# Residuals from GpSimd to VectorE, and value products by column halves, in a fused attention, expert and MLP kernel

## The chip, the cores and the metric

One Trainium2 chip; the kernel runs on one core. The metric is device time in microseconds (us) of one execution. The engines are PE (TensorE matmul, with its weight loads as PEld), DVE (VectorE), ACT (ScalarE), POOL (GpSimd) and SP (SyncE, which issues DMAs).

## The reference

```python
# attention: q, k, v (2, 8, 576, 64)
scores = scale * np.matmul(q, k.transpose(0, 1, 3, 2))        # scale 1/8
psi_rel = np.log1p(np.abs(rel)); psi_i = np.log1p(np.maximum(pos[:, None], 1.0))
h = np.maximum((psi_rel / psi_i)[..., None] @ w1 + b1, 0.0)   # w1 (1, 32)
scores = scores + (h @ w2).transpose(2, 0, 1)[None]           # w2 (32, 8): one bias per head
attn = softmax(scores); x = attn @ v                          # to (1152, 512)
# top-1 experts: 8 experts, capacity 288, 512 -> 1024 -> 512
expert_idx = np.argmax(x @ w_gate, axis=1); gate_w = probs[np.arange(N), expert_idx]
# the first 288 tokens of each expert, in order: out[i] = gate_w[i] * (relu(x_e @ w1[e]) @ w2[e])
# MLP: 512 -> 2048 -> 512
h = x @ w_in; g = np.maximum(0.01 * h, h); return g @ w_out
```

All inputs are fp32, except that the MLP's weights come as 64-bit floats.

## The kernel before

**Pairs of high and low part.** Fp32 products are made from PE's fp32r format. A matrix is stored as a pair: a cast to fp32r (the high part) and the residual, the raw value minus its cast. Three kinds of pair matter here. `prep_k` (L229 to L240) makes a key tile K: one ACT cast (L235) of 64 rows, then two residual instructions (L238) into the other 64 rows. `prep_q` (L258 to L269) makes a query tile Q for one pair of heads; a letter of the string `QE` says which engines: A is ACT cast (L261) and POOL residual (L269), B is ACT cast and DVE residual (L266), C is DVE cast (L263) and POOL residual, D is both on DVE. `KHE` says the same for the four key tiles of the first batch: A is POOL, D is DVE. `wsplit` (L670 to L672) makes a weight block P of 128x1024: ACT cast (L671), then the residual (L672) on the engine that the call names.

**Attention.** The work is cut in units (b, c, p): batch, chunk of 128 query rows (c = 0 to 3, and the short chunk c = 4 with 64 rows, named NFULL) and pair of heads p. The ten (b, c) follow a list: (0,1), (0,0), (0,3), (1,3), (0,4), (0,2), (1,2), (1,1), (1,0), (1,4), with four p each, so n runs from 0 to 39. In iteration n PE makes the scores of unit n+1 (`qk`, L329, into the one PSUM tile St), the transposes of unit n (L362 to L368) and the value products of unit n-1 (`pv`). DVE adds the bias and takes the minimum (`ttr`, L341, called bias step below), ACT makes the exponential (L352), ACT or DVE copy the transposes out (L372 to L387). In the first 28 iterations the bias itself is made beside that: relus on ACT, DVE and POOL (L165 to L169), bias matmuls (L182), their copies (L193 on ACT, L195 on DVE), then a round through DRAM.

**Value products.** For a full chunk `pv` has, per key tile, two matmuls with 64 weight columns, one per head (L399). For the short chunk both heads' 64 query rows stand side by side in the moving operand, and one matmul with 128 weight columns per key tile makes all four quadrants (L402, the last key tile in L404), of which the two on the diagonal are used (`fin_a`).

**Other work of attention's end.** At n = 20 to 25 the conversion of MLP weights runs on DVE (`conv_op`: L685, L687, L689, three steps per block). At n = 36 and 37 the first two expert weight blocks are split by `wsplit`.

**Experts and MLP.** Two full blocks of tokens come first, the first with splits on DVE, the last (`big_last`, L1063) on POOL. Then the MLP runs over the tokens (`chunk`, L1206): 16 weight blocks in the order of `PO`, four up, four down, four up, four down. In an up step (`up_half`) PE makes the product (L856 to L858), ACT scales by 0.01 (L880), DVE takes the maximum (L881), ACT casts the result to hq (L888) and DVE makes its residual (L889). Between them DVE converts the weights of a later block (`next(cv)`, into the tile raw), and `wsplit` splits the block of two steps later. In a down step PE runs L1191 to L1193. Only the first call, `chunk(0, True)`, runs for these inputs, and `any_block` doesn't run.

Each engine runs its instructions in the order in which they are written in the program; where an instruction's input is not there, all that stands behind it on that engine waits.

Of the kernel before, what the change touches and what calls it, by code (L numbers as in the profile page):

```python
# [26 lines left out]
NFULL = S // 128  # L27
# [30 lines left out]
START = ["Q0 k0 k1", "q0 v0", "q1 K0 v1", "q2", "Q1 q3 v2", "", "K1", "k2", "v3 B3 k3", "", "", "", ""]  # L58
SG = ()
PX = ((),(0,1),(2,3),(),())  # L60
KHE = "ADAA"
RENG = ('DAAA', 'DADD', 'DAPD', 'DDDD', 'DDPA', 'DDAD')
RP = "355355535352525234144534444144444342"
EP = "111111111100011111111101110111111111"
TP = "0021211100000230323333333232021010103333"
VL, KL, KP = ((9, 9, 13, 12), (8, 9, 9, 10), (9, 10, 10, 11))
LA = 5
QE = "DACDCDDCCCCCCCCCDDDADADADADACADADCDCDDDD"
PF = (3, 8, 1, 14, 21, 28)
QUOTA = [2, 2, 2, 2, 2, 2, 2, 2, 2, 2, 1, 1, 1, 1, 1, 1, 1, 1, 1, 1, 1, 1, 1, 1, 2, 2, 1, 1]  # L70
CST_W = MO + 128 + 128 + 2 * E_N + NENT + 3
# [3 lines left out]
def tile_attention_moe_mlp(ctx, tc, qc, kc, vc, wpk, cst, ctok, cap, wm, wo, out):  # L75
    nc = tc.nc
# [314 lines left out]
    def pv(c, p, ATs, Vs, xp):  # L391
        V, vt, vd = Vs
        AT, AX_ = ATs
        if c < NFULL:
            for t in range(NFULL + 1):
                for j in range(2):
                    h = 2 * p + j
                    w, a = (V[:, t, 64 * h : 64 * h + 64], AT[:, j, 128 * t : 128 * t + 128]) if t < NFULL else (vd[:, p, 64 * j : 64 * j + 64], AX_)
                    nc.tensor.matmul(xp[64 * j : 64 * j + 64, p, :], w, a, start=t == 0, stop=t == NFULL)  # L399
        else:  # L400
            for t in range(NFULL):
                nc.tensor.matmul(xp[:, p, :], V[:, t, 128 * p : 128 * p + 128], AT[:, 0, 128 * t : 128 * t + 128],  # L402
                                 start=t == 0, stop=False)
            nc.tensor.matmul(xp[:, p, :], vt[:, 128 * p : 128 * p + 128], AX_[0:64], start=False, stop=True)  # L404

    def fin_a(c, rs, xp, last):
        xt = rt.tile([128, NP, 128], F32, name="xt", tag="xt", bufs=1)
# [256 lines left out]
    raws, Ps, xhls, regs = [], [], [], {}  # L664
# [95 lines left out]
    def hooks(n):  # L760
        if n == 1:
            setup_late()
        if n == 12:
            nc.vector.tensor_copy(capf, cpi[:, 0:1])
        if n in PF:
            prefill(srt, 3 * PF.index(n), 3)
        if n == 16:
            nc.sync.dma_start(sid.rearrange("(p a) c -> p a c", p=128), pat)
        if n == NB0 + 4:
            queue("acc0", route_acc(0, range(NCH)))  # L770
        if n == NB0 + 5:
            flush("acc0")
            queue("route0", route0())
            queue("first0", first0())
        if n == SC[0]:
            flush("route0")
        if n in SC:
            scatter(0, SC.index(n))
        if n in ACC1:
            queue("acc1", route_acc(1, [i for i in range(NFULL) if ACCN[i] == n]))  # L780
        if n - 1 in ACC1:
            flush("acc1")
        if n == RF + 1:
            flush("first0")
            regs["e0"] = nc.values_load(ints[0:1, 2:3], engines=[SP], min_val=0, max_val=E_N - 1)
            regs["x0"] = nc.values_load(ints[0:1, 3:4], engines=[SP], min_val=0, max_val=S)
        if n in (CV0 - 3, CV0 - 2, CV0 - 1):
            g_w64(n - CV0 + 3)
        k, odd = divmod(n - CV0 - 2, 2)
        if odd == 0 and 0 <= k < len(CVA):  # L790
            nc.sync.dma_start(wsc[CVA[k]], cvd[k])
            if k + 3 < len(CVA):
                g_w64(k + 3)
        if n == 36:
            for t, m in xtiles:
                if t % 2 == 0:
                    kr = p1.tile([128, 2, S], F32, name="x0r", tag="kr", bufs=KRB)
                x0.append(kr[:, t % 2, 0:DM])
                nc.sync.dma_start(x0[t][0:m], srt[sl_(regs["x0"] + 128 * t, m), 0:DM])
            copy_id(regs["x0"], 0, CAPB)  # L800
        if n in (33, 34, 36, 37):
            raws.append(wp.tile([128, 1024], F32, name="raw", tag="bs", bufs=5))
            wdma(wsrc(regs["e0"], len(raws) - 1), raws[-1])
        if n in (36, 37):
            Ps.append(wp.tile([128, 2, 1024], F32R, name="P", tag="G", bufs=3))
            wsplit(raws[n - 36], Ps[-1], nc.gpsimd)
        if n == 38:
            xhls.append(wp.tile([128, 2, NP, CAPB], F32R, name="xhl0", tag="G", bufs=3))
        if n in (38, 39):
            wdma(wsrc(regs["e0"], n - 34), raws[n - 38])  # L810
        if n >= 38:
            x_tr(n - 38, x0[n - 38], xhls[0])
        if n == N:
            route1a()
            scatter(1, 0)
            scatter(1, 1)

    def tail_part(fa):
# [243 lines left out]
        def big_last():  # L1062
            xbase, base = bval(0, 1, 1, [SP]), bval(0, 1, 2, [ACT, DVE, SP])  # L1063
            copy_id(xbase, base, CAPB)
            ne = bval(1, 0, 0, [SP])
            for j in range(8):
                big_step(j, base, nc.gpsimd)
                if j > 2:
                    wdma(wsrc(ne, j - 3), R8[j - 3])

# [133 lines left out]
        def chunk(c, first):  # L1204
            w = MCS[c]
            groups = [(t, min(128, w - 128 * t)) for t in range(-(-w // 128))]  # L1206
            cv = convs()
            PP = [Ds[i] if first and i < 2 else Ps[i % 4] for i in range(16)]
            if not first:
                for i in range(3):  # L1210
                    wdma(wsc[i], raws[i])
                yprep(c)
            for i in range(3, 5):
                conv_start(i)
            if not first:
                for i in range(2):
                    wsplit(raws[i], PP[i], nc.vector)
            for i in range(13):
                if i + 2 < 16:
                    wsplit(spare if first and i == 0 else raws[(i + 2) % 4], PP[i + 2], nc.gpsimd)  # L1220
                q = PO[i]
                if q < 8:
                    for g in (0, 2, 1, 3):
                        up_half(PP[i], 2 * q + g // 2, w // 2 * (g % 2), w // 2)
                        if g != 3:
                            next(cv, None)
                else:
                    for kk in range(2):
                        for t, n in groups:
                            down_tok(PP[i], 2 * (q - 8) + kk, t, n)  # L1230
                            if t == 0:
                                split_h()
                            if 2 * t + kk in DCV:
                                next(cv, None)
                if i == 5:
                    for t, n in groups:
                        nc.sync.dma_start(idg[0:n, t], sid[MOF[c] + 128 * t : MOF[c] + 128 * t + n].bitcast(I32))
            wsplit(raws[15 % 4], PP[15], nc.vector)
            for t, n in groups:
                for i in range(13, 16):  # L1240
                    for kk in range(2):
                        down_tok(PP[i], 2 * (PO[i] - 8) + kk, t, n)
                emit(t, n)
# [21 lines left out]
    for n in range(N + 1):  # L1265
# [9 lines left out]
        if n + 1 < N:  # L1275
            b, c, p = units[n + 1]
# [88 lines left out]
```

## Time and profile before

| | |
|---|---|
| median of 3 runs | 407.12 us (406.49 to 407.96) |
| profiled execution | 408.05 us, of which the span is 406.3 |
| PE busy | 375.9 us, 93% of the span |
| PEld busy | 312.6 us, 77% |
| DVE busy | 307.7 us, 76%, 733 instructions |
| ACT busy | 242.9 us, 60% |
| POOL busy | 139.1 us, 34%, 110 instructions |
| PE's granted clock | full but for three stretches, two of them inside the work |

By stage: attention to about 214 us, the experts to 282, the chunk to the end. From about 244 on PE is busy in 9 tenths or more of nearly every slice of the page. A row of a timeline gives the start, the duration, the engine, the line, the operation, out and in, the number of instructions, and in brackets how long the engine had been idle before and what ended that.

### The profile page before, as it was taken

How to read it: one execution, taken by the hardware profiler on the slowest of the kernel's cores; microseconds unless marked ns; L12 is line 12 of the kernel's file. 1: busy time of each engine (PE TensorE's matmuls, PEld its weight loads, DVE VectorE, ACT ScalarE, POOL GpSimd, SP SyncE). 2: the span in 40 equal slices, each digit the busy share in tenths (PEclk: the TensorE clock that was granted, in tenths of full speed). 3: DMA queues.
4: the chain of work that ended last, by engine and by line, in shares of the span. 5: the costliest groups of instructions: out<-in, count | busy, mean ns of one | idle time of the engine just before them, and what ended most of it. 6: DMA issues, size and time to landing. Idle time of an engine off the chain costs nothing. (4 is left out here: it accounts for less than half of the span.)

```text
span 406.3 us, 8427 instructions
## 1 busy us (share of the span) xinstructions
PE 375.9 (93%) x2990; PEld 312.6 (77%) x2990; DVE 307.7 (76%) x733; ACT 242.9 (60%) x522; POOL 139.1 (34%) x110
## 2 busy tenths in 40 slices
PE   4777999988999999999999999999999999899993
PEld 2234666756688888988889999998988778788872
DVE  5998989899854888899458972137899999999310
ACT  3857898788865878767654875556544222455100
POOL 1445857574101110212332206840242255222311
PEclk9999899999999999999998999999999999999997
DMA  7979599798879938889185299683243366530011
GB/s 180 320 235 322 157 330 313 274 297 250 216 236 262 353 135 233 224 253 250 46 236 201 69 327 343 217 289 114 106 173 127 106 207 206 209 106 2 19 59 51
DMA packets 34050, 81.79 MB, mean 201 GB/s; under 512 B 8427, under 2 KB 8811, under 8 KB 31952
## 3 DMA queue, kind: packets, MB, share of 16 engines
q1 hardware_dynamic: 32880, 78.70, 61.3%
q0 software_dynamic: 1120, 2.48, 1.7%
q8 instruction: 25, 0.41, 0.4%
q14 instruction: 25, 0.20, 0.2%
HBM read 59.11 MB, written 23.20 MB: 203 GB/s over the span
## 5 line engine op out<-in xcount | busy, mean ns | idle before, releaser
L341 DVE CUSTOM_DVE_ANT_0 sv<-St,bt 128x576 f32<-128x576 f32 x72 | 52.9, 750 | 30.8 <-PE St L329 18.8
L672 POOL TENSOR_TENSOR P<-raw,P 128x1024 fp32r<-128x1024 f32 x18 | 45.3, 2521 | 76.6 <-ACT P L671 63.5
L352 ACT ACTIVATE A<-sv,mx 128x576 f32<-128x576 f32 x72 | 59.3, 837 | 3.2 <-DVE mx L341 3.0
L329 PE MATMUL St<-K,Q 128*128 128x320 f32 (+1 forms) x320 | 53.6, 310 | 2.6 <-DVE mx L341 2.2
L329 PEld LDWEIGHTS St<-K,Q 128*128 128x128 f32 x320 | 43.9, 189 | 14.6 <-issue 8.4
L182 PE MATMUL pb<-Gt,WP 128*32 128x272 f32 (+17 forms) x352 | 42.1, 505 | 13.3 <-DVE Gt L165 7.5
L269 POOL TENSOR_TENSOR Q<-qr,Q 128x256 fp32r<-128x256 f32 x22 | 16.9, 769 | 99.9 <-ACT Q L261 62.1
L165 DVE TENSOR_SCALAR Gt<-WL,bp 128x400 f32<-128x400 f32 (+17 forms) x98 | 49.4, 563 | 0.1
L671 ACT CAST P<-raw 128x1024 fp32r<-128x1024 f32 x27 | 28.3, 1048 | 28.3 <-DVE raw L689 22.7
L362 PE MATMUL pt<-CS,A 128*128 128x128 f32 x288 | 41.5, 284 | 1.3 <-ACT A L352 0.8
L372 ACT COPY AT<-pt 128x512 f32<-128x512 f32 x40 | 23.3, 583 | 29.2 <-PE pt L362 28.9
L362 PEld LDWEIGHTS pt<-CS,A 128*128 128x128 f32 x288 | 38.1, 206 | 2.2 <-ACT A L352 1.3
L169 POOL TENSOR_SCALAR Gt<-WL,bp 128x528 f32<-128x528 f32 (+12 forms) x17 | 34.1, 2009 | 8.2 <-DVE Gt L165 7.3
L399 PE MATMUL xp<-AT,V 128*64 128x128 f32 x512 | 35.9, 284 | 0.0
L399 PEld LDWEIGHTS xp<-AT,V 128*64 128x64 f32 x512 | 28.0, 139 | 9.8 <-issue 9.5
L182 PEld LDWEIGHTS pb<-Gt,WP 128*32 128x32 f32 x352 | 12.4, 110 | 29.8 <-DVE Gt L165 14.7
L856 PE MATMUL g<-yhl,P 128*128 128x304 f32 x96 | 30.5, 318 | 3.9 <-DVE gfa L881 3.9
L193 ACT ACTIVATE bs<-pb,CS 128x288 f32<-128x288 f32 (+53 forms) x60 | 27.2, 500 | 10.1 <-PE pb L182 9.5
L1193 PE MATMUL ac<-P,hq 128*128 128x512 f32 (+1 forms) x80 | 31.5, 394 | 0.0
L1191 PE MATMUL ac<-P,hq 128*128 128x512 f32 (+1 forms) x80 | 31.5, 394 | 0.0
L1192 PE MATMUL ac<-P,hq 128*128 128x512 f32 (+1 forms) x80 | 31.5, 394 | 0.0
L889 DVE TENSOR_TENSOR hq<-gfa,hq 128x304 fp32r<-128x304 f32 x32 | 28.9, 902 | 1.4 <-ACT hq L888 1.4
(322 smaller groups left out, 907.4 us busy)
## 6 DMA issues: line engine op xcount, KB each, us to landing
bt<-scr SPq DMA_DIRECT2D x24, 576.0 KB, 6.0
w<-wo SPq DMA_DIRECT2D x13, 1024.0 KB, 5.0
scr<-bs SPq DMA_DIRECT2D x36, 295.5 KB, 4.2
raw<-wm SPq DMA_DIRECT2D x14, 512.0 KB, 6.2
w<-wm SPq DMA_DIRECT2D x10, 512.0 KB, 5.7
srt<-pre SPq DMA_DIRECT2D x6, 771.0 KB, 8.4
qr<-qc SPq DMA_DIRECT2D x16, 256.0 KB, 5.7
w64g<-wo SPq DMA_DIRECT2D x3, 1024.0 KB, 10.3
```

Of the source, the lines that this page charges most:

```text
L165: nc.vector.tensor_scalar(G, src, bp[:, g : g + 1], 0.0, op0=ALU.add, op1=ALU.max)
L169: nc.gpsimd.tensor_scalar(G, src, bp[:, g : g + 1], 0.0, op0=ALU.add, op1=ALU.max)
L182: nc.tensor.matmul(pb[32 * q : 32 * q + 32, 0 : hi - lo], W2, gs[:, q, lo:hi], start=True, stop=True)
L329: nc.tensor.matmul(St[:, o + lo : o + hi], Q[:, h - 2 * p, w, :], K[:, h - 2 * p, lo:hi], start=n == 0, stop=n == len(seq) - 1)
L341: nc.vector.tensor_tensor_reduce(out=sv, in0=St, in1=bt[:, jb], scale=-0.125, scalar=3.0e38, op0=ALU.add, op1=ALU.min, accum_out=mx)
L352: nc.scalar.activation(A[:, :, j], sv, AF.Exp, bias=mx, scale=-1.0, accum_out=rs[:, col : col + 1])
L362: nc.tensor.transpose(pt[:, 128 * t : 128 * t + 128], A[:, 128 * t : 128 * t + 128, j], ident)
L399: nc.tensor.matmul(xp[64 * j : 64 * j + 64, p, :], w, a, start=t == 0, stop=t == NFULL)
L672: eng.tensor_tensor(out=P_[:, 1], in0=raw, in1=P_[:, 0].bitcast(F32), op=ALU.subtract)
L1191: nc.tensor.matmul(ps, hh, wh, start=k == 0, stop=False)
L1192: nc.tensor.matmul(ps, hh, wl, start=False, stop=False)
L1193: nc.tensor.matmul(ps, hl, wh, start=False, stop=k == F2 // 128 - 1)
```

## The change

The strings `KHE` and `QE` move residuals of keys and queries from POOL to DVE: three of the four key tiles (two instructions each) and 22 query tiles, 8 of which (A to B) stay behind an ACT cast and 14 (C to D) behind a DVE cast. Three calls of `wsplit` or its user name DVE in place of POOL: the two blocks at n = 36 and 37, the eight of the last full block, 13 in the chunk. POOL keeps its share of the bias relus, memsets, copies of tokens and DMAs. And the short chunk's `pv` has two matmuls per key tile, one per head, with 64 weight and 64 moving columns, into the two quadrants that are used. Lines from L403 on have a number higher by 2 afterwards.

```diff
-KHE = "ADAA"
+KHE = "DDDD"
...
-QE = "DACDCDDCCCCCCCCCDDDADADADADACADADCDCDDDD"
+QE = "DBDDDDDDDDDDDDDDDDDBDBDBDBDBDBDBDDDDDDDD"
...
         else:
-            for t in range(NFULL):
-                nc.tensor.matmul(xp[:, p, :], V[:, t, 128 * p : 128 * p + 128], AT[:, 0, 128 * t : 128 * t + 128],
-                                 start=t == 0, stop=False)
-            nc.tensor.matmul(xp[:, p, :], vt[:, 128 * p : 128 * p + 128], AX_[0:64], start=False, stop=True)
+            for t in range(NFULL + 1):
+                for j in range(2):
+                    r = slice(64 * j, 64 * j + 64)
+                    h = slice(128 * p + 64 * j, 128 * p + 64 * j + 64)
+                    w, a = (V[:, t, h], AT[:, 0, 128 * t + 64 * j : 128 * t + 64 * j + 64]) if t < NFULL else (vt[:, h], AX_[0:64, r])
+                    nc.tensor.matmul(xp[r, p, r], w, a, start=t == 0, stop=t == NFULL)
...
         if n in (36, 37):
-            wsplit(raws[n - 36], Ps[-1], nc.gpsimd)
+            wsplit(raws[n - 36], Ps[-1], nc.vector)
...
             for j in range(8):
-                big_step(j, base, nc.gpsimd)
+                big_step(j, base, nc.vector)
...
                 if i + 2 < 16:
-                    wsplit(spare if first and i == 0 else raws[(i + 2) % 4], PP[i + 2], nc.gpsimd)
+                    wsplit(spare if first and i == 0 else raws[(i + 2) % 4], PP[i + 2], nc.vector)
```

DVE at the front, around the third key tile: the query pair of a later unit (L263, L266), two bias copies (L195) and relus (L165) ahead of the bias step of the next unit (L341). Before:

```order
L387 COPY AX__427<-pt_424 128x128
L263 CAST Q<-qr 128x2x128
L266 TENSOR_TENSOR Q<-qr,Q 128x2x128
L195 TENSOR_SCALAR bs<-pb,CS 128x512
L195 TENSOR_SCALAR bs<-pb,CS 128x79
L165 TENSOR_SCALAR Gt<-WL,bp 128x480 x3
```

and after:

```order
L387 COPY AX__427<-pt_424 128x128
L263 CAST Q<-qr 128x2x128
L266 TENSOR_TENSOR Q<-qr,Q 128x2x128
L238 TENSOR_TENSOR K<-kr,K 64x576 x2
L195 TENSOR_SCALAR bs<-pb,CS 128x512
L195 TENSOR_SCALAR bs<-pb,CS 128x79
L165 TENSOR_SCALAR Gt<-WL,bp 128x480 x3
```

The two key residuals, which need ACT's cast L235, stand ahead of the bias copies and relus.

DVE beside the conversion (tile cvo) in attention. Before:

```order
L685 TENSOR_SCALAR cvo<-w64g 128x1024
L479 RECIPROCAL xn<-tm 64x1
L415 TENSOR_SCALAR rs<-rs 128x8
L687 SCALAR_TENSOR_TENSOR cvo<-w64g,cvo 128x1024
L417 RECIPROCAL rec<-rs 128x8
L341 ISA sv,mx<-St,bt 128x576
```

and after, with the same lines now two higher:

```order
L687 TENSOR_SCALAR cvo<-w64g 128x1024
L266 TENSOR_TENSOR Q<-qr,Q 128x2x128
L417 TENSOR_SCALAR rs<-rs 128x8
L689 SCALAR_TENSOR_TENSOR cvo<-w64g,cvo 128x1024
L419 RECIPROCAL rec<-rs 128x8
L341 ISA sv,mx<-St,bt 128x576
```

The query residual, behind an ACT cast, stands ahead of the second conversion step and of the bias step.

DVE in an up step of the chunk, between two blocks' conversions (tile raw). Before:

```order
L689 SCALAR_TENSOR_TENSOR raw<-w_3172,raw 128x1024
L881 TENSOR_TENSOR gfa<-g_3189,gfa 128x304
L889 TENSOR_TENSOR hq_3175<-gfa,hq_3173 128x304
L881 TENSOR_TENSOR gfa<-g_3190,gfa 128x304
L889 TENSOR_TENSOR hq_3175<-gfa,hq_3173 128x304
L685 TENSOR_SCALAR raw<-w_3171 128x1024
```

and after:

```order
L691 SCALAR_TENSOR_TENSOR raw<-w_3212,raw 128x1024
L883 TENSOR_TENSOR gfa<-g_3229,gfa 128x304
L891 TENSOR_TENSOR hq_3215<-gfa,hq_3213 128x304
L674 TENSOR_TENSOR P_3210<-raw,P_3210 128x1024
L883 TENSOR_TENSOR gfa<-g_3230,gfa 128x304
L891 TENSOR_TENSOR hq_3215<-gfa,hq_3213 128x304
L687 TENSOR_SCALAR raw<-w_3211 128x1024
```

The weight residual (now L674) stands one pair of maximum and residual behind the conversion's last step, ahead of the next pair.

## Rows read from the trace of the kernel before

**Rows 1.** Stretches: length, busy us (x) of PE, PEld, DVE, ACT, POOL; PEclk, DMA, GB/s

```profile
40.00:45.00 5.00, 4.96 (x37) 2.50 (x38) 4.96 (x13) 3.56 (x9) 4.90 (x4) 0.66 0.61 200
...
80.00:90.00 10.00, 8.50 (x94) 5.99 (x94) 9.93 (x26) 9.34 (x20) 7.74 (x7) 1.00 1.01 302
...
130.00:140.00 10.00, 10.00 (x74) 9.22 (x74) 6.88 (x25) 7.97 (x23) 1.21 (x2) 1.00 0.89 307
...
282.70:313.40 30.70, 28.71 (x192) 27.01 (x193) 28.00 (x42) 16.70 (x38) 9.61 (x4) 1.00 0.42 153
...
341.20:371.70 30.50, 28.52 (x194) 26.94 (x193) 29.98 (x39) 14.58 (x32) 10.28 (x4) 1.00 0.40 140
```

**Rows 2.** Groups by line and form: busy us, mean ns | idle before, releasers

```profile
L672 POOL TENSOR_TENSOR P<-raw,P 128x1024 fp32r<-128x1024 f32 x18 | 45.3, 2521 | 76.6 <-ACT P L671 63.5 <-DVE raw L685 7.0 <-PE ac L1193 6.0
...
L672 DVE TENSOR_TENSOR P<-raw,P 128x1024 fp32r<-128x1024 f32 x9 | 10.9, 1219 | 3.0 <-ACT P L671 1.8 <-DMA out<-pre 1.2
...
L266 DVE TENSOR_TENSOR Q<-qr,Q 128x256 fp32r<-128x256 f32 x18 | 7.6, 424 | 0.3
...
L238 DVE TENSOR_TENSOR K<-kr,K 64x576 fp32r<-64x576 f32 x2 | 1.4, 748 | 0.1
```

**Rows 3.** Timeline of the chunk: start, us, engine, what, [idle before <-releaser]

```profile
301.28 1.05 ACT L671 CAST P<-raw 128x1024 fp32r<-128x1024 f32 x1 [1.12 <-DVE raw L689]
...
301.51 0.45 DVE L889 TENSOR_TENSOR hq<-gfa,hq 128x304 fp32r<-128x304 f32 x1
...
302.41 2.40 POOL L672 TENSOR_TENSOR P<-raw,P 128x1024 fp32r<-128x1024 f32 x1 [5.95 <-ACT P L671]
...
303.08 2.06 DVE L889 TENSOR_TENSOR hq<-gfa,hq 128x304 fp32r<-128x304 f32 x1
```

**Rows 4.** Groups of the weight conversion's third step, two tiles

```profile
L689 DVE SCALAR_TENSOR_TENSOR raw<-w,raw 128x1024 uint32<-128x1024 uint32 x13 | 24.1, 1857 | 0.2
...
L689 DVE SCALAR_TENSOR_TENSOR cvo<-w64g,cvo 128x1024 uint32<-128x1024 uint32 x3 | 3.6, 1214 | 0.0
```

**Rows 5.** Waits: us in total, times, longest; then PE at the first phase's end

```profile
PEld g L856 <- DVE gfa L881: 6.7, 13, 1.2
...
312.31 0.30 PE L857 MATMUL g<-yhl,P 128*128 128x304 f32 x1
...
313.42 0.39 PE L1191 MATMUL ac<-P,hq 128*128 128x512 f32 x1
```

**Rows 6.** Timeline of the last units of attention

```profile
200.73 1.05 ACT L671 CAST P<-raw 128x1024 fp32r<-128x1024 f32 x1
...
201.11 0.76 DVE L341 CUSTOM_DVE_ANT_0 sv<-St,bt 128x576 f32<-128x576 f32 x1 [1.99 <-PE St L329]
...
205.36 0.76 DVE L341 CUSTOM_DVE_ANT_0 sv<-St,bt 128x576 f32<-128x576 f32 x1 [2.54 <-PE St L329]
```

**Rows 7.** Timeline beside the conversion in attention

```profile
147.41 0.44 ACT L261 CAST Q<-qr 128x256 fp32r<-128x256 f32 x1
...
147.95 0.76 DVE L341 CUSTOM_DVE_ANT_0 sv<-St,bt 128x576 f32<-128x576 f32 x1 [0.25 <-ACT Q L261]
```

**Rows 8.** Timeline of the front

```profile
36.53 0.95 DVE L195 TENSOR_SCALAR bs<-pb,CS 128x512 f32<-128x512 f32 x2
...
37.46 1.15 ACT L235 CAST K<-kr 64x1152 fp32r<-64x1152 f32 x1 [2.28 <-DMA kr<-kc]
...
40.04 1.75 PE L182 MATMUL pb<-Gt,WP 128*32 128x480 f32 x8 [2.11 <-ACT bs L193]
...
40.43 0.74 DVE L341 CUSTOM_DVE_ANT_0 sv<-St,bt 128x576 f32<-128x576 f32 x1
```

**Rows 9.** Timeline of value products, PE and its weight loads

```profile
129.81 1.06 PE L402 MATMUL xp<-AT,V 128*128 128x128 f32 x8
...
148.88 0.85 PEld L399 LDWEIGHTS xp<-AT,V 128*64 128x64 f32 x16 [0.17 <-issue]
...
148.88 1.09 PE L399 MATMUL xp<-AT,V 128*64 128x128 f32 x16
```

## The prediction

> **What bounds the kernel now.** I read the table of busy time by stretch first, because the mean over the span (PE 93%, DVE 76%, POOL 34%) mixes stages with different limits. In the attention stretch 130 to 140 us PE is busy all of the 10.00 us and DVE 6.88 [rows 1]: there a shorter matmul step is worth its whole length and a DVE instruction is free. In 80 to 90 it is the other way round: DVE 9.93, PE 8.50 [rows 1]. In the expert chunk, between 282.7 and 313.4 and between 341.2 and 371.7, PE is at 28.71 of 30.70 and 28.52 of 30.50 and DVE at 28.00 and 29.98 [rows 1]: neither is free, and in the second of them DVE is as good as full. The busy time of DVE is then to be taken apart, since part of it is not work. The second view, the groups of instructions by line, gives each operation's price on either engine [rows 2]. The third, the timeline of the chunk, shows what DVE's figure hides: the residual of hq (L889) takes 0.45 us at 301.51, but 2.06 at 303.08, when POOL's residual (L672) runs from 302.41 for 2.40 [rows 3]. It ends at 305.14, just after POOL's end at 304.81. The weight conversion shows the same: L689 takes 1214 ns in the group whose tile is cvo and 1857 in the group whose tile is raw; 13 x 0.643 = 8.4 us more in all [rows 4]. So a DVE instruction with its operands in SBUF waits for a POOL residual to end, and pays nearly its whole length.
>
> The Trainium skill (SBUF — State Buffer, "Who interferes with whom") calls the port pair that DVE and GpSimd share an exclusive lock; the two rows of L889 agree, with 0.45 and 2.06 us. By it every move from POOL to DVE would be a gain wherever DVE works anyway, the early residuals too, which I do not take over, because those wait for ScalarE.
>
> **The change part by part.**
>
> Weight residuals, 23 that run: 13 in the chunk, 8 in the last full block, 2 in the last units of attention. On POOL one is 2.52 us in the mean, on DVE 1.22 [rows 2]. In the chunk, first up phase, four POOL residuals lie over it. Worked through at the one of 302.41: the cast on ACT begins at 301.28 and takes 1.05 [rows 3], so the residual can start on DVE at 302.33; the pair of sum and residual of hq ahead of it (the L889 of 301.51) is through at 301.96, so DVE waits 0.4; the residual lasts to 303.55 and the next pair, two instructions like the one of 0.45, to 304.5, against 305.14 now: 0.65 an instance, 2.6 in four. PE's weight loads wait 6.7 us for the sum gfa (L881) in 13 waits, and eight matmuls take 1.11 us at full rate (312.31 to 313.42), 0.139 each [rows 5]. With 192 matmuls per phase the floor is 26.7; the phase takes 30.7, so at most 4.0 can go. I take 1.7 of the 2.6, since the sum behind the moved residual comes later than now within its step. In the down phase between them PE sets the pace; DVE loses 8.4 us [rows 4] and so begins the second up phase late. Four residuals of 1.22 put 4.9 in place of 8.4: DVE arrives 3.5 earlier. In the second up phase DVE is full [rows 1], so this and its own smaller stretches come through, up to PE's floor, 30.5 - 26.7 = 3.8. I take 3.3. Chunk: -5.0, between -6.5 (most of 4.0 + 3.8) and -1.5 (below). What is late next there is the ACT cast (L671, 1.05), for which the DVE residual now has to wait in line, with the sums of the chunk behind it.
>
> The 8 residuals of the last full block: the first full block has its splits on DVE already, and from about 244 us on PE is busy in 9 tenths of nearly every slice, so 9.8 us more on DVE find room; I take 0, with +-0.5.
>
> The two residuals at n = 36 and 37 now stand on DVE ahead of two bias steps (L341). The first cast runs at 200.73 for 1.05 and ends at 201.78; the residual then ends at 203.0, while the bias step behind it had begun at 201.11 [rows 6]: 1.9 late. The exponential and then the next cast follow it on ACT, so that lag passes to the second residual, which stands ahead of the bias step of 205.36 [rows 6]. PE's transposes wait for those steps, but DVE had itself been idle 2.54 before 205.36, waiting for PE, so I take half: +1.0, between 0 and +2 (1.9, rounded). This also swallows what the value products gain in these units.
>
> Query residuals, 22 at 0.42 on DVE [rows 2] = 9.3 us. The 14 behind DVE's own cast cost only their length: in the written order four of them stand in the stretch that 80 to 90 stands for, where DVE is the bound, 1.7 us; POOL's query residuals no longer hold DVE there, by up to their own length each, which I set against it: 0, between -1 and +1. Eight stand behind a cast on ACT. Three of these meet a weight conversion: the cast at 147.41 runs 0.44, to 147.85, and the bias step begins at 147.95, with a conversion step of 1.21 [rows 4] already done [rows 7]. In the new order the residual comes before that conversion step, so DVE stands until 147.85 and does 0.42 + 1.21 before the bias step: near 149.5 instead of 147.95, 1.6 late. Three times is 4.8; PE has other units' work in between and I take 1.5 in all, between 0 and +3.
>
> Key residuals, six instructions at 0.75 [rows 2]: three tiles. The third shows the danger. DVE reaches it about 36.5, behind a query residual, where it now starts L195 (36.53) [rows 8]. The ACT cast for this tile, which itself waited for its load, begins at 37.46 and takes 1.15, to 38.61; two residuals bring DVE to 40.1, and L195, the bias relus and the bias step at 40.43 come 2.7 to 3.6 later. PE was idle 2.11 just before 40.04 [rows 8] and ran at a granted clock of 0.66 on average between 40 and 45 (half rate for most of it) [rows 1], so some of this lag falls into time already lost, and in the PE-bound stretch behind it DVE catches up. I take +1.0 for the three tiles, between 0 and +4.6 (rival 1).
>
> Value products of the short chunk, eight units (four in the stretch of 130, four near 205). Before, 8 records of 128 weight columns take 1.06 us (129.81) [rows 9]; after, 16 records of 64 weight columns and 64 moving columns. The same count with 128 moving columns (L399) takes 1.09 on PE and 0.85 in its weight loads (148.88) [rows 9]. A unit is between -0.5 (half of everything, 0.53) and +0.03 (L399's own time), and the switch of output quadrants, which no row of before prices, I bound by one record of the 16, +0.07. Nearest is L399, whose weights have the same size; with half of its moving columns the loads are what is left: 0.85 against 1.06, -0.2 a unit. Four units in the PE-bound stretch: -0.8, between -2.0 and +0.4. Here the Trainium skill speaks against the change: TensorEngine Tiling (Array Packing), "Instruction Overhead", says not to take a tiling factor from a dimension that is already small, and "Key Properties" that a change of tiling mode drains TensorE. By those the sum for this part would be at or above zero; no row here shows a drain priced. The L399 units have the same column tiling already and stand at 1.09 per 16.
>
> Sum: -5.0 + 0 + 1.0 + 0 + 1.5 + 1.0 - 0.8 = **-2.3 us**. It is made against the profiled execution (408.05, span 406.3), which is 0.93 above the median of the three runs, 407.12 (406.49 to 407.96). Applied to the median: **404.8**.
>
> **The rivals.**
>
> 1. The key waits stop the front of the pipeline. Decided at 36.5 to 44: if PE's bias matmuls (40.04) start later than about 42, then the lag of DVE (2.9) stays and the clock's half-rate spell comes a second time; by the 0.66 over 5 us one costs 1.7. That is 4.6 in place of 1.0: sum +1.3, and the half of the query waits that I let PE absorb is then no longer covered (+1.0): +2.3, **409.4, slower**. For it: a cast that waits for its load, on an in-order engine, with everything behind it. Against: PE's idle 2.11 there and DVE's slack afterwards.
>
> 2. The chunk gives back what it gains: DVE's freed time is spent waiting for ACT's cast, with L881 and L889 behind it. Decided by the idle time of DVE before the moved residual: at 0.4 us or less per step the forecast holds, at 1.2 the whole of DVE's gain is gone in the up phases; only 1.5 is left. Sum +1.2: **408.3, no change**. For it: ACT's cast comes directly behind the conversion (L671 at 301.28 ended an idle time of 1.12 that L689 released [rows 3]), so the residual is never early. Against: one pair of sum and residual stands between conversion and moved residual in the written order and covers two thirds of the cast.
>
> 3. The value halves give nothing or cost: loads one after another as in L399, and the switch, 4 x (0.03 + 0.07) = +0.4 instead of -0.8: **406.0**, at the border of no change. For it: L399 stands at 1.09 with the same weights. Against: its moving columns are twice as many. It is how the rule of the Trainium skill named above (TensorEngine Tiling (Array Packing), "Instruction Overhead") would come true here.
>
> 4. The waits in attention are all covered, by PE's work on other units: 0 in place of 1.0 + 1.5 + 1.0, sum -5.8: **401.3**. For it: PE has work queued between 130 and 140 without a gap. Against: each of these waits stands ahead of a bias step, and St is one tile.
>
> **How the numbers follow.** Forecast 0.40, rival 1 0.18, rival 2 0.18, rival 3 0.12, rival 4 0.12. A measurement of this kernel can tell about 0.3% (1.2 us) from no change: faster is below 405.9, slower above 408.3. The forecast's own spread (402.8 to 406.8) puts 0.33 of its 0.40 on faster and the rest on same; rival 4 is faster; rival 3 is split 0.06 to 0.06; rival 2 is 0.03 faster, 0.10 same, 0.05 slower; rival 1 is 0.03 same and 0.15 slower. Together faster 0.54, same 0.26, slower 0.20. The range runs from 401.0 (just under rival 4) to 409.6 (just over rival 1), which leaves out the outer halves of those two and some more, about 0.2.
>
> **What would show it.** In the chunk: L889 and L689 at 0.45 and 1.21 throughout, the two up phases at 29.0 and 27.2 us, DVE's wait for L671 under 0.5 each. At 36 to 44: a wait of DVE for L235, and PE's L182 with 480 columns starting before 42. At 147: a wait of DVE for L261 near 1.4. At 200 to 208: a wait for L671 ahead of two bias steps. At 129 to 138: 16 records at 0.85. A chunk gain under 2 us, or a second stretch of half clock before 60 us, makes the prediction wrong.

## The result, and the profile after

The changed kernel is slower. Over nine runs each its median is 410.0 us (407.67 to 411.61) and that of the kernel before 407.81 us (405.84 to 408.99); the ratio is 1.0054, with a 95% interval from 1.0028 to 1.0079, so about +2.2 us. The forecast was -2.3, and the median lies just above the range's upper end, 409.6.

The profiled execution spans 407.5 us (before 406.3). Both programs run the same score matmuls and weight products on PE in the same order, so their starts can be laid side by side, which tells where the lag is made. The times are read from the two timelines of PE.

| place on PE | before | after | lag |
|---|---|---|---|
| scores of unit 18 (before the short chunk's products) | 123.81 | 125.79 | +1.98 |
| scores of unit 22 (behind four units of them) | 138.06 | 138.56 | +0.50 |
| scores of unit 28 (behind the conversion) | 162.30 | 166.32 | +4.02 |
| scores of unit 39 | 203.88 | 207.76 | +3.88 |
| first product of the experts | 214.33 | 220.48 | +6.15 |
| first product of the last full block | 244.35 | 251.43 | +7.08 |
| first product behind that block | 269.83 | 276.91 | +7.08 |
| first down product of the chunk | 313.42 | 318.40 | +4.98 |
| last down product | 398.82 | 400.07 | +1.25 |

The gains are there: 1.5 us in the value products and 5.8 from the end of the last full block to the end of the chunk. The losses are larger: 2.0 in the front, 3.5 beside the conversion, and 3.2 between unit 39 and the last full block. The first lines below are the groups of the changed kernel by line and form; the columns are as in [rows 2], and the lines answer to [rows 2] and [rows 4].

```profile
L674 DVE TENSOR_TENSOR P<-raw,P 128x1024 fp32r<-128x1024 f32 x27 | 32.9, 1222 | 15.3 <-ACT P L673 14.4 <-DMA sid<-srt 0.9
...
L266 DVE TENSOR_TENSOR Q<-qr,Q 128x256 fp32r<-128x256 f32 x40 | 17.6, 440 | 12.2 <-ACT Q L261 11.6
L691 DVE SCALAR_TENSOR_TENSOR raw<-w,raw 128x1024 uint32<-128x1024 uint32 x13 | 15.9, 1220 | 0.1
L891 DVE TENSOR_TENSOR hq<-gfa,hq 128x304 fp32r<-128x304 f32 x32 | 14.9, 465 | 0.0
...
L238 DVE TENSOR_TENSOR K<-kr,K 64x576 fp32r<-64x576 f32 x8 | 5.7, 749 | 2.8 <-ACT K L235 2.7
```

The hold is gone: the conversion's third step (now L691) takes 1220 ns where it took 1857, and the residual of hq (now L891) 465 in the mean where it took 902. What has come instead stands behind the bars: DVE is idle 11.6 us ahead of query residuals, waiting for ACT's cast L261, and 14.4 ahead of weight residuals. Of the 14.4 only 2.6 lie in the chunk. The timeline of DVE there, the place of [rows 3], shows why.

```profile
305.12 1.22 DVE L691 SCALAR_TENSOR_TENSOR raw<-w,raw 128x1024 uint32<-128x1024 uint32 x1
306.26 0.47 DVE L883 TENSOR_TENSOR gfa<-g,gfa 128x304 f32<-128x304 f32 x1
306.64 0.47 DVE L891 TENSOR_TENSOR hq<-gfa,hq 128x304 fp32r<-128x304 f32 x1
307.46 1.22 DVE L674 TENSOR_TENSOR P<-raw,P 128x1024 fp32r<-128x1024 f32 x1 [0.35 <-ACT P L673]
308.60 0.47 DVE L883 TENSOR_TENSOR gfa<-g,gfa 128x304 f32<-128x304 f32 x1
308.99 0.46 DVE L891 TENSOR_TENSOR hq<-gfa,hq 128x304 fp32r<-128x304 f32 x1
```

The wait is 0.35 (forecast 0.4); over the 13 residuals of the chunk it is between 0 and 0.51. The first up phase lasts from 289.45 to 318.40, 28.95 us (forecast 29.0), the second from 346.11 to 372.91, 26.80 (forecast 27.2; PE's floor was put at 26.7). PE's waits for the maximum, 6.7 in 13 in [rows 5], are down to two:

```profile
PEld g L858 <- DVE gfa L883: 1.3, 2, 0.7
```

The same kind of wait is dear in attention. This is DVE of the changed kernel beside the conversion, the place of [rows 7]:

```profile
147.50 0.68 DVE L687 TENSOR_SCALAR cvo<-w64g 128x1024 uint32<-128x1024 uint32 x1
149.51 0.43 DVE L266 TENSOR_TENSOR Q<-qr,Q 128x256 fp32r<-128x256 f32 x1 [1.33 <-ACT Q L261]
149.86 0.27 DVE L457 TENSOR_TENSOR lw<-pl,rec 64x64 f32<-64x64 f32 x1
149.99 1.21 DVE L689 SCALAR_TENSOR_TENSOR cvo<-w64g,cvo 128x1024 uint32<-128x1024 uint32 x1
151.12 0.20 DVE L465 TENSOR_REDUCE lg<-lw 64x8 f32<-64x64 f32 x1
151.25 0.74 DVE L341 CUSTOM_DVE_ANT_0 sv<-St,bt 128x576 f32<-128x576 f32 x1
```

DVE stands 1.33 us, and then the residual, the conversion step and small work run before the bias step at 151.25. At 140.39 and 158.86 it waits 1.49 and 1.91 in the same way. And PE, whose rows of the same stretch follow, waits in its turn: for a reciprocal (L419) that stands behind the first of these residuals, then for the bias step (the row names L469, a small step of DVE that ends right behind it) and for the exponential.

```profile
142.22 0.28 PE L432 MATMUL pr<-rs,CS 128*64 128x4 f32 x2 [0.77 <-DVE rs L419]
...
152.89 1.30 PE L329 MATMUL St<-K,Q 128*128 128x320 f32 x8 [0.78 <-DVE tm L469]
154.88 1.23 PE L362 MATMUL pt<-CS,A 128*128 128x128 f32 x8 [0.69 <-ACT A L352]
```

Not all of these waits are dear. At 120.47, 126.47, 133.06 and 167.68 DVE stands 2.11, 1.48, 1.62 and 1.42 us for the same cast, but no conversion step stands between those residuals and the next bias step, and there the lag over the kernel before doesn't grow: it is +1.97 at units 16 and 17, the 1.48 gained from unit 18 to unit 22 is what the halves gain alone (below), and it is +4.02 at unit 28 and +4.03 at unit 29.

Near the end of attention, the place of [rows 6], the two weight residuals stand ahead of their bias steps, as told; PE's row is the one that pays:

```profile
205.81 1.23 DVE L674 TENSOR_TENSOR P<-raw,P 128x1024 fp32r<-128x1024 f32 x1 [2.69 <-ACT P L673]
206.95 0.75 DVE L341 CUSTOM_DVE_ANT_0 sv<-St,bt 128x576 f32<-128x576 f32 x1
...
209.84 1.23 DVE L674 TENSOR_TENSOR P<-raw,P 128x1024 fp32r<-128x1024 f32 x1 [1.23 <-ACT P L673]
210.98 0.75 DVE L341 CUSTOM_DVE_ANT_0 sv<-St,bt 128x576 f32<-128x576 f32 x1
```

```profile
212.77 0.74 PE L362 MATMUL pt<-CS,A 128*128 128x128 f32 x4 [1.64 <-ACT A L352]
```

PE is idle 1.64 before 212.77, and then it works at half rate for longer. In the table by stretch (columns as in [rows 1]) the granted clock of the changed kernel is:

```profile
212.00:216.00 4.00, 3.23 (x34) 2.54 (x36) 1.85 (x9) 1.94 (x6) 0.00 (x0) 0.78 0.82 330
216.00:220.00 4.00, 4.00 (x34) 3.27 (x32) 3.35 (x18) 1.85 (x6) 0.00 (x0) 0.50 0.24 77
220.00:224.00 4.00, 4.00 (x24) 3.66 (x24) 3.17 (x13) 1.49 (x3) 0.99 (x1) 0.50 0.92 352
```

and of the kernel before, in the same stretches:

```profile
212.00:216.00 4.00, 3.29 (x25) 2.90 (x26) 3.57 (x19) 1.89 (x4) 0.00 (x0) 0.78 0.93 327
216.00:220.00 4.00, 4.00 (x26) 3.93 (x26) 3.48 (x16) 1.06 (x5) 1.02 (x1) 0.79 0.57 219
220.00:224.00 4.00, 4.00 (x33) 4.00 (x32) 3.02 (x10) 2.74 (x5) 2.02 (x2) 1.00 0.17 66
```

The value products themselves, the place of [rows 9], gained more than was forecast. The rows of PE and of its loads in the changed kernel, with the last key tile as the second pair:

```profile
128.43 0.55 PEld L406 LDWEIGHTS xp<-AT,V 128*64 128x64 f32 x16 [0.20 <-issue]
128.43 0.69 PE L406 MATMUL xp<-AT,V 128*64 128x64 f32 x16
129.04 0.19 PEld L406 LDWEIGHTS xp<-AX__1723,vt 64*64 64x64 f32 x4
129.04 0.33 PE L406 MATMUL xp<-AX__1723,vt 64*64 64x64 f32 x4
```

Sixteen records take 0.69 us where eight took 1.06. The prediction held a rule of the Trainium skill (TensorEngine Tiling (Array Packing), "Instruction Overhead") against the change; in these rows the step from 128 to 64 columns is a gain all the same, and no run shows at how few columns it would stop being one.

### The profile page after: what moved, and what is told of

It is laid out like the page before. It is cut to its first block, busy times and chain, and to the rows that moved or that the text cites. A ratio compares the mean times of both kernels' runs of the same rounds, so it can differ in the third digit from the quotient of the medians.

```text
span 407.5 us, 8521 instructions
## 1 busy us (share of the span) xinstructions
PE 373.2 (92%) x3070; PEld 310.6 (76%) x3070; DVE 313.1 (77%) x784; ACT 243.4 (60%) x522; POOL 54.8 (13%) x59
## 5 line engine op out<-in xcount | busy, mean ns | idle before, releaser
L341 DVE CUSTOM_DVE_ANT_0 sv<-St,bt 128x576 f32<-128x576 f32 x72 | 52.6, 747 | 11.9 <-PE St L329 7.9
L182 PE MATMUL pb<-Gt,WP 128*32 128x272 f32 (+17 forms) x352 | 41.6, 495 | 13.1 <-DVE Gt L165 10.6
L674 DVE TENSOR_TENSOR P<-raw,P 128x1024 fp32r<-128x1024 f32 x27 | 32.9, 1222 | 15.3 <-ACT P L673 14.4
L165 DVE TENSOR_SCALAR Gt<-WL,bp 128x400 f32<-128x400 f32 (+17 forms) x98 | 40.2, 470 | 0.1
L182 PEld LDWEIGHTS pb<-Gt,WP 128*32 128x32 f32 x352 | 12.7, 111 | 29.7 <-DVE Gt L165 19.1
L858 PE MATMUL g<-yhl,P 128*128 128x304 f32 x96 | 29.4, 306 | 0.8 <-DVE gfa L883 0.8
L859 PE MATMUL g<-yhl,P 128*128 128x304 f32 x96 | 29.0, 302 | 0.0
L860 PE MATMUL g<-yhl,P 128*128 128x304 f32 x96 | 28.9, 301 | 0.0
```

Source lines behind the costliest of these rows:

```text
L165: nc.vector.tensor_scalar(G, src, bp[:, g : g + 1], 0.0, op0=ALU.add, op1=ALU.max)
L182: nc.tensor.matmul(pb[32 * q : 32 * q + 32, 0 : hi - lo], W2, gs[:, q, lo:hi], start=True, stop=True)
L341: nc.vector.tensor_tensor_reduce(out=sv, in0=St, in1=bt[:, jb], scale=-0.125, scalar=3.0e38, op0=ALU.add, op1=ALU.min, accum_out=mx)
L674: eng.tensor_tensor(out=P_[:, 1], in0=raw, in1=P_[:, 0].bitcast(F32), op=ALU.subtract)
```

## The experiments

Ratios are to the kernel before on the same chip, with their 95% intervals; one hundredth of the time is 4.1 us. A half-rate stretch of PE falls at different places in different executions (below), so one trace alone settles no term under 2 us, and the verdicts rest on the timed runs.

**The parts alone.** Halves of the value products in the kernel before (the diff is that of `pv`):

> The kernel before with the value products of the short chunk in two column halves, and nothing else. In the trace of the changed kernel a unit goes from about 1.5 to 1.0 us of PE. Theory A: eight units of 0.5, of which the four between 125 and 140 come through whole (-2.0) and the four near 205 in part: 404.3 to 405.8, ratio 0.991 to 0.995. The prediction on record had -0.8 for it: ratio 0.998. Theory B (the gain is given back by a later wait): ratio 1.000.

Measured: 0.9971 (0.9948 to 0.9994), -1.2 us. Theory A's -2.0 for the first four units is too much: their trace gains 1.48 from unit 18 to unit 22, as in the changed kernel, and 0.44 of that is lost again at the next unit, where PE waits 0.25 for ACT's exponential.

```diff
-                    wsplit(spare if first and i == 0 else raws[(i + 2) % 4], PP[i + 2], nc.gpsimd)
+                    wsplit(spare if first and i == 0 else raws[(i + 2) % 4], PP[i + 2], nc.vector)
```

> The kernel before with the 13 weight residuals of the chunk on DVE, and nothing else. Theory A: DVE's instructions are no longer held by POOL's residuals; -5.0 to -5.8 us, ratio 0.986 to 0.988, with L689 at 1.21 and L889 at 0.45 throughout. Theory B (a wait for the ACT cast takes the place of the hold): ratio 0.996 to 1.000.

Measured: 0.9892 (0.9856 to 0.9928), -4.4 us (-5.9 to -2.9). Its up phases last 29.67 and 26.80 us on PE (before 30.73 and 30.45), with L689 at 1.22 and L889 at 0.47 in the mean. Theory A, if a little less than it said; theory B's range lies outside the interval.

```diff
-QE = "DACDCDDCCCCCCCCCDDDADADADADACADADCDCDDDD"
+QE = "DBDDDDDDDDDDDDDDDDDBDBDBDBDBDBDBDDDDDDDD"
```

> The kernel before with the query residuals of the changed kernel (22 from POOL to DVE), and nothing else. Theory A: three waits of DVE for ACT's cast, 1.3 to 1.9 us each, with a conversion step and the bias steps behind them, cost 3.5 us between 138 and 163, and the added work in the stretch where DVE is the bound up to 2: +3.5 to +5.5, ratio 1.009 to 1.013. Theory B (the lag in the changed kernel's trace there comes from the half-rate stretch that lies at 91 instead of 40, not from the queries): ratio 1.000 to 1.003.

Measured: 1.0126 (1.0100 to 1.0152), +5.1 us. Theory A. The lag grows from 1.43 at unit 22 to 4.57 at unit 28, beside the conversion, and its waits there are those of the changed kernel:

```profile
DVE Q L266 <- ACT Q L261: 6.1, 4, 1.9
```

```diff
-KHE = "ADAA"
+KHE = "DDDD"
```

> The kernel before with its four key tiles' residuals of the first batch on DVE, and nothing else. Theory A (the trace of the changed kernel, where the scores of units 3 to 8 come 0.4 to 0.6 later than before, shows all of it): +0.2 to +0.6, ratio 1.000 to 1.002. The prediction on record: +1.0, ratio 1.0025, and its first rival +4.6, ratio 1.011.

Measured: 1.0036 (1.0015 to 1.0057), +1.5 us. The forecast's +1.0 lies inside; what I had read from the trace of the changed kernel (0.2 to 0.6) is too small. This run's trace has PE at half rate from 14.4 to 17.8 and from 41.7 to 45.1, that of the changed kernel at neither place, and that of the kernel before from 40.2 to 43.6; whether the difference comes from that isn't shown.

```diff
-            wsplit(raws[n - 36], Ps[-1], nc.gpsimd)
+            wsplit(raws[n - 36], Ps[-1], nc.vector)
```

> The kernel before with the two weight residuals at n = 36 and 37 on DVE, and nothing else. Theory A (two waits of DVE ahead of bias steps, with PE waiting behind them and a longer half-rate stretch): +2 to +4.5, ratio 1.005 to 1.011. The prediction on record: +1.0, ratio 1.0025. Theory B (they cost that much only together with the halves, which empty PE's queue there): ratio 1.000 to 1.002.

Measured: 1.0047 (1.0031 to 1.0063), +1.9 us, just below theory A's range and twice the forecast's term.

```diff
 def big_last():
-                big_step(j, base, nc.gpsimd)
+                big_step(j, base, nc.vector)
```

> The kernel before with the eight weight residuals of the last full block on DVE, and nothing else. Theory A (PE is full there and hides them): ratio 0.998 to 1.001. Theory B (DVE's waits for the casts reach PE): above 1.002.

Measured: 1.0005 (0.9988 to 1.0022). Theory A: free.

The six parts sum to -1.2 - 4.4 + 5.1 + 1.5 + 1.9 + 0.2 = +3.1 us; the whole change measured +2.2 (1.1 to 3.2). Nothing beyond the parts is needed.

**The parts undone in the changed kernel.** The weight residuals at n = 36 and 37 back on POOL:

> The changed kernel with the two weight residuals at n = 36 and 37 back on POOL, and nothing else. In the trace of the changed kernel DVE waits 2.69 and 1.23 us for their casts, PE then 1.64 for an exponential, and PE's half-rate stretch that begins near 214 lasts to 224 instead of 218. Theory A (the waits are the cause, and PE's idle time is what prolongs the half rate): -2.5 to -3.5 against the changed kernel, ratio to the kernel before 0.997 to 0.9995, and half rate near 214 as short as before. The prediction on record had 1.0 for it: ratio 1.003. Theory B (the long half-rate stretch has another cause): ratio 1.003 to 1.005 with half rate still to 224.

Measured: 0.9991 (0.9965 to 1.0017), which is 2.6 us below the changed kernel's 1.0054. Half rate at this place lasts from 219.3 to 222.7, 3.4 us, as long as before. Theory A.

The eight query residuals behind an ACT cast back on POOL (each B of `QE` made an A):

> The changed kernel with the eight query residuals behind an ACT cast back on POOL; the fourteen behind DVE's own cast stay on DVE. Theory A (the waits for ACT's cast cost 3.5 us between 138 and 163): ratio to the kernel before 0.996 to 0.998. Theory B (it is the added work on DVE in the front, which stays here): 1.003 to 1.006.

Measured: 0.9978 (0.9953 to 1.0003), 3.1 us below. Theory A. Its trace loses 0.43 from unit 22 to unit 28, where the changed kernel loses 3.52.

**Order or work.** First, the same eight residuals on DVE one iteration later:

```diff
+        if QE[k] == "B" and k >= NP:
+            qlate.append((Q, qr))
...
             sv = ttr(*units[n + 1][1:], st, bts[n + 1])
+            q_flush()
```

> The changed kernel with the eight query residuals behind an ACT cast still on DVE, but written one iteration later, behind the next unit's bias steps, when the cast is long done (the first of the start is left where it is). The work on DVE is the same. Theory A (the place in the order costs, not the work): as with these residuals on POOL, ratio to the kernel before 0.996 to 0.998, with no wait of DVE for L261. Theory B (the 0.42 us each cost, or ACT is behind by then too): 1.002 to 1.006.

Measured: 1.0028 (1.0003 to 1.0054). By its own terms this is theory B; theory A's range lies outside the interval. None of the moved residuals waits for its cast any more, yet only about 1 us of the 3.1 is back. The trace shows where the rest is. From unit 22 to unit 28 about two thirds of the loss are gone (table below). But from unit 29 to unit 30 this run takes 4.63 us where the run with these residuals on POOL takes 3.57. Each residual of a query pair also lets one step of small deferred work be written behind it (`tick`); moved with the residual, a step of the experts' gate on ACT (L480 in this run), which waits 1.02 for DVE, now stands ahead of the exponential, and PE waits 0.80 for that exponential. So the later place removed one wait and made another.

Next, the wait was tried with hardly any work:

```diff
+        if QE[k] == "A":
+            nc.vector.tensor_copy(dm, Q[:, 0, 0, 0:1].bitcast(F32))
```

> The changed kernel with the eight query residuals behind an ACT cast on POOL, but with a DVE copy of one column that waits for the same cast in the place where each residual stood: the wait without the work (nobody reads the copy). Theory A (the wait and its place in the order cost, not the 0.42 us): as the changed kernel, 1.003 to 1.006 of the kernel before, with the waits of 1.3 to 1.9 us near 140, 149 and 158. Theory B (the work costs): as with them on POOL and no copy, 0.996 to 0.999.

> The same without the copies (the eight query residuals on POOL), once more beside it: 0.996 to 0.999.

Measured: 1.0061 (1.0036 to 1.0085) with the copies, 0.9972 (0.9953 to 0.9990) without. Copies of one column cost 3.6 us, about as much as the residuals themselves, and DVE's waits are those of the changed kernel:

```profile
141.87 0.15 DVE L267 COPY dm<-Q 128x1 f32<-128x1 f32 x1 [1.50 <-ACT Q L261]
...
151.26 0.16 DVE L267 COPY dm<-Q 128x1 f32<-128x1 f32 x1 [1.36 <-ACT Q L261]
151.33 0.27 DVE L461 TENSOR_TENSOR lw<-pl,rec 64x64 f32<-64x64 f32 x1
151.47 1.66 DVE L693 SCALAR_TENSOR_TENSOR cvo<-w64g,cvo 128x1024 uint32<-128x1024 uint32 x1
...
160.78 0.15 DVE L267 COPY dm<-Q 128x1 f32<-128x1 f32 x1 [1.92 <-ACT Q L261]
```

The copies are not quite the wait alone. POOL's residual starts at the same cast, and one DVE step behind each of these three copies is longer by about half a us (L693 takes 1.66 at 151.47 and 1.21 otherwise, a small step behind the other two 0.67 and 0.73 where it takes 0.16 without the copies); that is as long as the 0.42 us of a residual. And each copy brings its `tick` with it, as the residual did. The stretch from unit 22 to unit 28, in which PE's granted clock is 1.00 in every one of these traces, sets the runs side by side:

| kernel | unit 22 to unit 28, us |
|---|---|
| before | 24.24 |
| changed | 27.76 |
| before, with all 22 query residuals on DVE | 27.38 |
| changed, with the eight on POOL (two runs) | 24.67 and 24.66 |
| the same with the copies | 28.50 |
| changed, with the eight one iteration later | 25.63 |

So the loss belongs to these eight residuals and their place, and no residual on DVE is needed for it: a wait for ACT's cast in this place with half a us behind it is enough. With the work but without the waits 0.96 of the 3.1 is left here, so the waits are the larger part; a run with the wait and nothing else there is lacking.

The two weight residuals behind their bias steps instead of ahead of them:

```diff
-            wsplit(raws[n - 36], Ps[-1], nc.vector)
+            nc.scalar.copy(Ps[-1][:, 0], raws[n - 36])
+            plate.append((Ps[-1], raws[n - 36]))
...
             sv = ttr(*units[n + 1][1:], st, bts[n + 1])
         if n < N:
+            p_flush()
```

> The changed kernel with these two residuals still on DVE, but each written directly behind the bias step that it stood ahead of; its cast is then a whole bias step older. Theory A (the place in the order costs, not the 1.22 us of work): as with them on POOL, ratio to the kernel before 0.998 to 1.000, DVE's wait for their cast under 0.5 and no wait of PE for the exponential of this unit. Theory B (DVE's work there costs wherever it stands): 1.003 to 1.006.

Measured: 0.9946 (0.9927 to 0.9964): the whole change becomes faster than the kernel before by moving two instructions by one place. The timeline of DVE in this run:

```profile
205.63 0.76 DVE L347 CUSTOM_DVE_ANT_0 sv<-St,bt 128x576 f32<-128x576 f32 x1 [1.95 <-PE St L335]
206.31 0.20 DVE L425 RECIPROCAL rec<-rs 128x8 f32<-128x8 f32 x1
206.43 1.18 DVE L277 TENSOR_TENSOR P<-raw,P 128x1024 fp32r<-128x1024 f32 x1
...
209.14 0.76 DVE L347 CUSTOM_DVE_ANT_0 sv<-St,bt 128x576 f32<-128x576 f32 x1 [0.94 <-PE St L335]
```

The residual begins at 206.43 without a wait, with the bias step before it, and the next bias step waits for PE again, not for it. That it is also better than POOL (0.9991) did not hold on the faster kernel, next.

**The parts that gain.** Halves, last block and chunk on DVE; queries, keys and the two residuals as before:

> The changed kernel without its waits in attention: keys, queries and the two weight residuals at n = 36 and 37 as before, and only the value products by halves, the residuals of the last full block and those of the chunk on DVE. Theory A (the chunk and the halves gain what the trace of the changed kernel shows, 5.5 and 4 times 0.5 us, and DVE's waits behind ACT casts in attention, 3.5 and some 3 us, ate it): 407.8 - 5.5 - 2 to -3.5, so 399 to 401, ratio 0.980 to 0.984. Theory B (what is gained at one place comes back as a longer stretch at half clock or as a later wait, wherever it is gained): 404 to 407.

Measured: 0.9843 (0.9815 to 0.9871), median 402.3 us, at the upper edge of theory A's ratios; theory B's times lie outside the interval. It beats both kernels. With the two residuals on DVE behind the bias steps, and once more without:

> Halves, last block and chunk on DVE, queries and keys as before, and the two weight residuals at n = 36 and 37 on DVE directly behind the bias steps instead of ahead of them. Theory A (in its place behind the bias step a residual on DVE is better than on POOL, as the run with the changed kernel showed by 0.45%): 0.979 to 0.983 of the kernel before. Theory B (that run's better ratio came from elsewhere): 0.983 to 0.987, as without it.

> The same with these two residuals on POOL, once more beside it: 0.982 to 0.987.

Measured: 0.9844 (0.9816 to 0.9871) and 0.9833 (0.9807 to 0.9860), medians 401.56 and 401.54: no difference. With the fourteen query residuals behind DVE's own cast on DVE as well:

> The kernel with halves, last block and chunk on DVE (the first of these runs, ratio 0.984), and also the fourteen query residuals that stand behind DVE's own cast on DVE. Nothing waits for another engine in them; only their 0.42 us each are added, and POOL's hold on DVE goes. Theory A (work alone, hidden or set off by the hold): 0.983 to 0.986. Theory B (they cost their length where DVE leads, four to six of them): 0.987 to 0.992.

Measured: 0.9869 (0.9826 to 0.9911). This can't be told from 0.984, and theory B, which needs 0.987 or more, isn't excluded either; it stays open.

## Why the prediction was wrong

| term | forecast, us | alone, us |
|---|---|---|
| chunk | -5.0 | -4.4 |
| value products by halves | -0.8 | -1.2 |
| last full block | 0 | +0.2 |
| key residuals | +1.0 | +1.5 |
| two residuals at n = 36, 37 | +1.0 | +1.9 |
| query residuals | 0 + 1.5 | +5.1 |
| sum | -2.3 | +3.1 |

**Right.** That DVE's instructions pay for POOL's residuals, and what each phase of the chunk gains (29.0 and 27.2 forecast, 28.95 and 26.80 in the trace), with the ACT cast as the next late thing but at 0.35 an instance: rival 2 fell. That the last block is free (the lag is +7.08 ahead of it and behind it). That the value products gain; the step from the loads (0.85) was too cautious, the trace has 0.69 with loads of 0.55, and rival 3 fell. That DVE would wait for L235 near 36.5 and PE's L182 with 480 columns would start before 42: DVE waited 0.64 and was through with the residuals at 39.9, and the matmuls started at 41.34, with 1.10 of waiting for DVE's relus, so rival 1 didn't come either. The waits of DVE were named at their places and with their sizes: 1.4 for L261 near 147 (1.33, 1.49, 1.91), and the two ahead of bias steps near 205.

**Wrong: the term of the query residuals**, the step that took 1.5 of 4.8 because "PE has other units' work in between". It rested on the sentence on [rows 1] that in 130 to 140 "a DVE instruction is free" (DVE busy 6.88, PE 10.00). That PE is full says that nothing waits for DVE as the kernel stands; it doesn't say how late DVE may be. St is one tile: PE can't make the next scores before the bias step has read it, and has one unit's transposes and value products to do meanwhile. In the kernel before PE began these scores at 150.12 without a wait; in the changed kernel it waits 0.78 and 0.69 for the same chain. Of the 4.8 us that I had counted, 3.5 came through, not 1.5; of the 5.4 us between the two sums of the table, 3.6 are this term's. The argument was in the prediction against its own fourth rival ("St is one tile"), and wasn't applied to the forecast. The mechanism, waits behind ACT's cast that a conversion step follows, was right, and so was the choice of the three places; what was mis-sized is how much of it PE would absorb.

The other part of this term, 0 for the fourteen residuals behind DVE's own cast, is less sure: 5.1 alone less the 3.1 of the eight leaves 2.0, but added to the faster kernel they cost nothing that the runs can tell. There the forecast's reason for 0 is seen: DVE's relus (L165) take 512 ns in the mean with them and 568 without, 5.4 us less in all, against 5.9 us for fourteen residuals of 0.42.

**Wrong in size: the two residuals at n = 36 and 37**, 1.0 against 1.9 alone and 2.6 inside the changed kernel. Here too I took half of the lag as absorbed, from DVE's idle 2.54 before 205.36 [rows 6]. And I left out that PE's idle time there is followed by half rate: the stretch from 214.3 lasts to 217.7 before, to 224.5 after, and 3.4 us again with the two residuals on POOL. With the residuals on DVE it wasn't long each time (216.5 to 219.9 in the run with this part alone), so the half rate would fit with the part costing more in the whole change than alone. But its length doesn't go by these residuals only: in the run of the parts that gain, with both on POOL, it lasts from 210.9 to 217.7, and in the changed kernel with the eight query residuals on POOL from 209.8 to 223.5. No run separates it from the wait.

The range's upper end (409.6) was made from the key residuals' rival, a case that didn't come. The one that did, 3.5 at the queries, lies above the term's own bound, "between 0 and +3".

**Not separated: the clock.** Over its nine runs the changed kernel's granted clock is 0.977 in the mean, and that of the kernel before, beside the experiments, 0.989. The difference is 0.012 of 408 us, 4.9 us of full-rate time. That is an estimate of the most that the lower clock can cost, since it costs less wherever PE isn't what sets the pace; but it is more than the 2.2 us to be explained, so what part of the whole slowdown is paid at half rate stays open. The cost of the eight query residuals doesn't hang on it: the stretch from unit 22 to unit 28 ran at 1.00 in every trace, and the runs with the copies and those without, as compared above, have the same clock, 0.977.

## What to carry to other kernels

An instruction moved to an in-order engine can cost the wait for its input, and that wait is paid by everything written behind it: eight copies of one column that waited for another engine's casts cost 3.6 us, while two weight residuals of 1.22 us each, moved from ahead of a bias step to behind it, turned the change from 1.0054 to 0.9946. Waits just as long, with no long step between them and the next bias step, cost nothing that the trace shows. Before a step is moved, ask when its input is ready relative to its place, and place it behind the instruction that another engine is waiting for; and see what small work moves with it. A busy share says that an engine has free time, not how late it may be: here a single tile, St, stood between DVE and PE.

## What the runs showed of the hardware that I had not expected

- PE's half-rate stretches (granted clock 0.50, the lower of its two levels) move between executions of nearly the same program. In the profiled executions they lie, ahead of the last microseconds, at 40.2 to 43.6 and 214.3 to 217.7 (before), at 91.4 to 94.8 and 214.3 to 224.5 (after), at 31.2 to 34.6 and 212.1 to 215.5 (halves alone), and at 31.0, 95.9, 215.3 and 283.6 (chunk alone). Three that were looked at follow a place where PE idles: it stood still for 2.11 us before 40.04 (before), was busy 1.38 of the 3.40 us from 88.0 to 91.4 and idle for 1.64 before 212.77 (after). Where exactly, and how many there are, differs, and the single runs of the kernel before spread over 405.84 to 411.23 us.
- Sixteen records with 64 weight and 64 moving columns take 0.69 us, 43 ns each, and their loads 0.55; with 128 moving columns they take 1.09 and 0.85 [rows 9]. So the loads, too, got shorter beside shorter matmuls, which the forecast had taken as fixed.
